# Gated linear attention and a bilinear feed-forward network on one core: blocks of 256 tokens by two rows, full-width loads, two states per block, gaps and two chunks' decay by matmuls, a reordered start

## The chip, the core and the metric

The kernel runs on one core of one Trainium2 chip. The metric is the device time of one execution in microseconds (us). A run is called fast if it lies within 1.5% of the fastest of its kernel, and only fast runs are compared. The profile is of one execution; its span is shorter than the time of the same execution, by 1.7 us for the kernel before (232.1 against 233.83).

TensorE does the matmuls, VectorE, ScalarE and GpSimd the elementwise work, SyncE and GpSimd issue the loads. Sixteen DMA engines carry the data. Each engine works through its instructions in order; that matters for everything below (in the changed kernel ScalarE stands 8.40 us for one late load, with ready work behind it).

## The reference

```python
for t in range(S):                                  # B=4, H=8, S=768, D=48
    state = alpha[:, :, t, :, None] * state + einsum('bhd,bhe->bhde', k[:, :, t], v[:, :, t])
    y[:, :, t] = einsum('bhd,bhde->bhe', q[:, :, t], state)
x = y.transpose(0, 2, 1, 3).reshape(3072, 384)
return (x @ w_a) * (x @ w_b) @ w_out                # 384 -> 1536 -> 384
```

The kernel computes the recurrence in blocks: the logarithm of alpha, a prefix sum of it by matmul, scaled keys and queries, masked scores inside a block, and a state carried from block to block. In the text a *chunk* is 512 tokens, of which there are six. Its feed-forward part is 24 groups of three 128x512 matmuls and an output product of 48 matmuls (`ff_a`, `ff_b`, `ff_o`). The schedule places the attention of chunk c+1 between the feed-forward groups of chunk c, by hand.

## The kernel before: what the change touches

The schedule is a list of stages for the start, and for each chunk a list of (step, chunk, stage): the stage is emitted behind that feed-forward group. `ld` loads, `L` is the logarithm, `A` the prefix sum and its exponentials, `dec` brings the decay at a block's end to the state's layout, `mk`/`mq` scale keys and queries, `C` transposes, `D` makes the masked scores, `Y` is the product with the values, `K` updates the state, `v` casts the values, `W`/`Wo` load weights. The letter at the end names the engine (V VectorE, P GpSimd, S ScalarE, Y SyncE).

```python
START = [ ...
    (0, "ld k 1 YP"), (0, "ld q 1 YP"), (0, "ld v * YP"), ...
    (0, "gate_w k"), (0, "W 0 256"), (0, "W 256 768"), (0, "W 768 1536"),    # weights wait for chunk 0's k
    (1, "gate_in a"), (1, "ld a * YP"), (1, "ld k 0 YP"), (0, "Wo 0 4"), ...   # then chunk 1
    (0, "ff 0 0"), (0, "ff 1 0"), (0, "Y 1 S dma"), (0, "ff 2 0"), ... ]
def _steady(c):
    n, m = c + 1, c + 2
    return _ld(0, m) + [(0, n, "C 0 0 V"), ... (18, n, "Y 1 S dma"), (18, n, "fill YY"), (20, n, "K 1"),
            (18, m, "L * P"), ... (25, m, "dec"), ...]
...
def load(ch, what, us, engs):                       # two DMAs, 64 partitions each
    for g in range(2):
        bs = slice(2 * g + us.start, 2 * g + us.stop)
        engs[g].dma_start(out=t[g * HC:(g + 1) * HC, us]..., in_=src[bs, :, ch.c * C:(ch.c + 1) * C, :]...)
...
def stY(ch, u, eng, how="dma"):
    if ch.c > 0:                                    # state product: full-array, block-diagonal state
        for p in range(P2):
            for g in range(2):
                nc.tensor.matmul(y[:, g, p, :], lhsT=Sb[:, 2 * g + u, p, :], rhs=..., ...)
    ...
    if ch.c > 0 and how == "pe":                    # gap rows by matmul (chunk 1 only)
        evac(KT, P2); ...; evac(0, KT)
def fill(ch, engs):                                 # gap rows by DMA (later chunks)
    for t in range(KT):
        for r in range(2):
            engs[r].dma_start(out=ch.xT[r * DP + D:(r + 1) * DP, t], in_=ch.xT[r * DP + t * G:..., KT])
```

(Cuts are marked by dots.) The heads are 48 wide and lie in tiles of 64 rows; the 16 "gap" rows are filled from the fourth pair of heads, so that three full 128-row tiles make the 384 columns of x.

## Time and profile before

| | kernel before |
|---|---|
| median of 4 runs | 233.28 us (231.94 to 233.68) |
| span of the profiled run | 232.1 us |
| TensorE busy | 205.6 us, 89% |
| first feed-forward group of chunk 0 | 23.54 us |
| first full-width group of chunk 1 | 70.69 us |
| steady period of a chunk | 31.95 us |

The two times in the middle: the first says when TensorE's main work begins, the second (I call it T1) when the start is over.

### The profile page before, as it was taken

What the parts mean: (1) busy time and instruction counts of PE and PEld (TensorE: products, weight loads), DVE (VectorE), ACT (ScalarE), POOL (GpSimd) and SP (SyncE); (2) the same over time, 40 slices, a digit from 0 to 9 for tenths busy, and PEclk for the clock granted to TensorE, in tenths of its full rate; (3) what the DMA queues carried; (4) which work ended last, traced back from release to release, by engine and by line L of the source; (5) the groups of instructions that cost most, each with busy time, mean ns of one, the idle gap of its engine ahead of it and who ended that gap; (6) DMA issues with size and microseconds to landing.
All of it is one profiled execution on the core that took longest, in us unless ns stands there. A gap on an engine that the chain in (4) does not pass through costs nothing.

```text
span 232.1 us, 5488 instructions
## 1 busy us (share of the span) xinstructions
PE 205.6 (89%) x2238; PEld 116.2 (50%) x2238; DVE 119.6 (52%) x174; ACT 120.1 (52%) x192; POOL 86.3 (37%) x96
## 2 busy tenths in 40 slices
PE   6488499497998879996999989999899999999992
PEld 6366364234664345562555555465455555644461
DVE  2676337335424758715588641977625875035500
ACT  3568334865537843838234777344793344234420
POOL 7558784157003890145901079202477000000000
PEclk9759979979999999999799999999999999999998
DMA  6999999995999319992399811699723000230023
GB/s 134 228 193 107 142 179 202 233 221 75 176 208 215 85 4 197 203 192 74 57 207 205 121 48 36 120 199 204 114 54 87 0 3 9 68 79 0 0 55 82
DMA packets 61584, 27.93 MB, mean 120 GB/s; under 512 B 53668, under 2 KB 60984, under 8 KB 61560
## 3 DMA queue, kind: packets, MB, share of 16 engines
q1 hardware_dynamic: 54440, 20.91, 54.5%
q0 software_dynamic: 5008, 5.90, 15.3%
q10 hardware_dynamic: 2112, 0.79, 1.9%
q8 instruction: 17, 0.28, 0.5%
q14 instruction: 7, 0.06, 0.1%
HBM read 25.98 MB, written 4.75 MB: 132 GB/s over the span
## 4 chain that ended last, share of the span: by engine, by line
PE 60%; DMA 16%; SPq 8%; ACT 5%; issue 4%; POOL 4%; DVE 1%; ACTq 0%; POOLq 0%; DVEq 0%
PE f L360 19%; PE f L351 15%; PE f L343 14%; SPq L164 6%; DMA v_t<-in_v_dram 5%; DMA k_t<-in_k_dram 4%; PE f L229 3%; PE s L247 3%; DMA wb_t<-in_moe_w_b_dram 2%; DMA wa_t<-in_moe_w_a_dram 2%; PE y L260 2%; PE y L266 2%; PE f L200 2%; DMA a_t<-in_alpha_dram 1%; ACT la L178 1%
## 5 line engine op out<-in xcount | busy, mean ns | idle before, releaser
L351 PE MATMUL f<-xT,wb_t 128*128 128x512 bf16 (+1 forms) x225 | 61.5, 384 | 2.8 <-DMA wb_t<-in_moe_w_b_dram 2.8
L343 PE MATMUL f<-xT,wa_t 128*128 128x512 bf16 (+1 forms) x225 | 60.6, 378 | 3.4 <-DMA xT<-xT 2.0
L360 PE MATMUL f<-wo_t,prod 128*128 128x384 bf16 x288 | 49.5, 326 | 1.4 <-ACT as__2133 L345 0.6
L360 PEld LDWEIGHTS <-prod 128*128 128x128 bf16 x288 | 27.8, 98 | 21.8 <-issue 2.9
L343 PEld LDWEIGHTS <-wa_t 128*128 128x128 bf16 x225 | 22.3, 100 | 29.3 <-DMA xT<-xT 3.2
L248 DVE TENSOR_TENSOR m<-s,mask 128x1024 bf16<-128x1024 f32 x22 | 26.9, 1223 | 15.7 <-PE s L247 15.7
L351 PEld LDWEIGHTS <-wb_t 128*128 128x128 bf16 x225 | 19.9, 101 | 21.5 <-issue 5.0
L326 POOL TENSOR_TENSOR Sb<-tmp,bl 48x384 bf16<-48x384 f32 x16 | 14.7, 918 | 37.6 <-DVE tmp L325 37.0
L362 ACT ACTIVATE ot<-f 128x384 f32<-128x384 f32 x24 | 11.8, 491 | 28.3 <-PE f L360 28.1
L208 POOL TENSOR_TENSOR Kp<-k_t,invb 128x768 bf16<-128x768 f32 x10 | 18.1, 1814 | 18.1 <-ACT invb L204 7.7
L200 PE MATMUL f<-l,ut_f 128*128 128x384 f32 x24 | 12.8, 619 | 7.5 <-DVE l L180 6.9
L208 POOL TENSOR_TENSOR Qp<-q_t,beta 128x768 bf16<-128x768 f32 x10 | 18.5, 1847 | 0.0
L235 DVE COPY qk<-f 128x1024 bf16<-128x1024 bf16 x16 | 11.1, 692 | 14.0 <-PE f L229 13.9
L180 POOL TENSOR_TENSOR l<-la 128x768 f32<-128x768 f32 x4 | 7.3, 1813 | 23.5 <-ACT la L178 23.5
L287 ACT ACTIVATE xT<-y 128x1024 bf16<-128x1024 f32 (+2 forms) x14 | 12.2, 872 | 6.0 <-PE y L260 4.8
L201 DVE TENSOR_TENSOR le<-f,la 128x384 f32<-128x384 f32 x12 | 6.7, 557 | 15.8 <-PE f L200 15.6
L325 DVE TENSOR_TENSOR tmp<-s,Sb 48x384 f32<-48x384 f32 x16 | 8.9, 555 | 7.0 <-PE s L315 6.4
L229 PE MATMUL f<-ident,Qp 128*128 128x128 bf16 x96 | 10.0, 230 | 2.4 <-POOL Qp L208 2.1
L178 ACT ACTIVATE la<-a_t 128x1536 f32<-128x1536 f32 (+1 forms) x7 | 9.1, 1302 | 4.4 <-DMA a_t<-in_alpha_dram 4.3
L247 PEld LDWEIGHTS <-qk 64*64 64x64 bf16 x384 | 6.6, 109 | 8.1 <-issue 3.1
L229 PE MATMUL f<-ident,Kp 128*128 128x128 bf16 x96 | 9.8, 227 | 0.7 <-DVE Kp L208 0.7
L247 PE MATMUL s<-qk 64*64 64x128 bf16 x352 | 9.3, 225 | 0.9 <-ACT qk L233 0.7
(219 smaller groups left out, 265.7 us busy)
## 6 DMA issues: line engine op xcount, KB each, us to landing
out_dram<-ot SPq DMA_DIRECT2D x48, 96.0 KB, 2.2
k_t<-in_k_dram SPq DMA_DIRECT2D x20, 192.0 KB, 6.4
q_t<-in_q_dram SPq DMA_DIRECT2D x20, 192.0 KB, 7.4
v_t<-in_v_dram SPq DMA_DIRECT2D x9, 384.0 KB, 8.3
a_t<-in_alpha_dram SPq DMA_DIRECT2D x9, 384.0 KB, 5.0
wo_t<-in_moe_w_out_dram POOLq DMA_DIRECT2D x3, 384.0 KB, 13.6
k_t<-in_k_dram POOLq DMA_DIRECT2D x3, 192.0 KB, 9.2
q_t<-in_q_dram POOLq DMA_DIRECT2D x3, 192.0 KB, 11.8
```

What stands on the lines that cost most here:

```text
L164: engs[g].dma_start(out=t[g * HC:(g + 1) * HC, us].rearrange("p b h r d -> p (b h) (r d)"), in_=src[bs, :, ch.c * C:(ch.c + 1) * C, :].rea ...
L200: nc.tensor.matmul(p, lhsT=ut_f32, rhs=ch.l2[:, u].rearrange("p h d -> p (h d)"), start=True, stop=True)
L208: eng.tensor_mul(dst[ch.c % 2][:, u, :, :, :D], src[:, u].rearrange("p h r d -> p r h d"), by[:, u])
L229: nc.tensor.transpose(t[:, j, p, :, r, :], src[:, u, r, hp:hp + 2, :].rearrange("s h d -> s (h d)"), ident)
L247: nc.tensor.matmul(s2[g * HC:(g + 1) * HC, r, p, rk, :], lhsT=qk[rs, 1, p, g, rk * HC:(rk + 1) * HC], rhs=qk[rs, 0, p, g, :], start=True, ...
L248: nc.vector.tensor_mul(m.rearrange("p r a k s -> p (r a) (k s)"), s2.rearrange("p r a k s -> p (r a) (k s)"), maskn(4))
L287: nc.scalar.activation(out=o_, in_=i_, func=AF.Copy)
L326: nc.gpsimd.tensor_mul(so, tmp[rs], bl)
L343: nc.tensor.matmul(ap, lhsT=wa_t[:, kk, f * 128:(f + 1) * 128], rhs=ff_x(ch, us)[:, kk], start=(kk == 0), stop=(kk == KT - 1))
L351: nc.tensor.matmul(bp, lhsT=wb_t[:, kk, f * 128:(f + 1) * 128], rhs=ff_x(ch, us)[:, kk], start=(kk == 0), stop=(kk == KT - 1))
L360: nc.tensor.matmul(op, lhsT=ch.prod[:, f, m * C:(m + 1) * C], rhs=wo_t[:, f, :], start=(f == 0), stop=(f == NFF - 1))
L362: nc.scalar.activation(out=ot, in_=op, func=AF.Copy)
```

## The change

Its intent: loads of the full 128 partitions, an earlier start of chunk 1, fewer zeros in the state products, no small DMAs on the path, and scalings on the faster engine. The core of the diff, with cuts:

```diff
 START = [
-    (0, "ld a 0 YS"), ... (0, "gate_w k"), (0, "W 0 256"), ..., (1, "gate_in a"), (1, "ld a * YP"), ...
+    (0, "new"), (0, "ld a 0 Y"), (0, "L 0 V"), (1, "new"), (0, "ld a 1 Y"), (0, "ld q 0 Y"), (1, "gate_in a 0"), (0, "ld k 0 Y"), ...
+    (0, "ld v 0 Y"), (0, "ld k 1 Y"), ... (0, "ld v 1 Y"), (0, "W 0 512"), ... (1, "gate_in k 1"),
+    (0, "W 512 1536"), (1, "ld a * Y"), (0, "Wo 8 12"), ... (1, "ld q * Y"), (0, "dec P"), (1, "ld k * Y"), ...
+    ... (0, "C 1 0 V"), (0, "D 1 0 s2"), (0, "K 1 P y2"), (0, "ff 0 0"), (0, "S 1"), ...
 PLAN:
+    0: [(0, 1, "L * V"), (6, 1, "A 0"), (8, 1, "A 1"), (8, 1, "mk 0 V"), ..., (11, 1, "dec P"), ...
+        (16, 1, "K * P"), (16, 2, "new"), (17, 2, "ld a * P"), ..., (22, 2, "ld k * P"), (26, 2, "ld v * P"), (26, 2, "A 1")],
+    1: [(1, 2, "mq 0 V"), ..., (5, 2, "dec D"), ..., (13, 2, "K * P"), ..., (15, 2, "S 0"), ...
 def load(...):
-    for g in range(2): engs[g].dma_start(out=t[g * HC:(g + 1) * HC, us]..., in_=src[bs, :, ch.c * C:..., :]...)
+    eng.dma_start(out=t[:, us]..., in_=src[ch.b0 + us.start:ch.b0 + us.stop, :, ch.s * 2 * C:(ch.s + 1) * 2 * C, :]...)
+def decay_pe(ch):            # decay of a block by one-column matmuls, for chunks 0 and 1
+    nc.tensor.matmul(s2[r * DP:r * DP + D, g, e:e + 1], lhsT=ch.l2[gs, u, hd, :], rhs=one[gs], ...)
+def stS(ch, u):              # state products, 64x64, first half from S0, second from Sm
+    nc.tensor.matmul(y[rs, g, p, :], lhsT=Sm[...] if g else S0[...], rhs=queriesT(ch, u, p, g, rs), ...)
+def stG(ch, u, eng):         # gap rows by matmul, for every chunk
-def fill(...)                # gone
```

Chunks 2 to 5 get their decay through DRAM (`dec D`): the row is written out, and read back in the state's layout.

## The prediction

> **What bounds the kernel now.** I read the page first: the busy shares, then its forty slices. The core's TensorE is busy 89% of the span, no other engine over 52%.
>
> ```profile
> PE 205.6 (89%) x2238; PEld 116.2 (50%) x2238; DVE 119.6 (52%) x174; ACT 120.1 (52%) x192; POOL 86.3 (37%) x96
> ...
> PE   6488499497998879996999989999899999999992
> ...
> DMA  6999999995999319992399811699723000230023
> GB/s 134 228 193 107 142 179 202 233 221 75 176 208 215 85 4 197 203 192 74 57 207 205 121 48 36 120 199 204 114 54 87 0 3 9 68 79 0 0 55 82
> ```
>
> The span has two parts. In the first ten slices (58 us) the DMA engines are full and TensorE has holes; later the DMA has holes and TensorE is full. The chain of work that ended last, in order of time, agrees: loads and their issues up to about 56 us, then almost only matmuls.
>
> ```profile
> 0.74 3.43 DMA a_t<-in_alpha_dram
> 4.19 9.77 DMA k_t<-in_k_dram
> ...
> 30.05 0.68 SPq L164
> 30.77 0.67 SPq L164
> 31.48 2.42 SPq L164
> 33.94 3.57 SPq L164
> 37.56 3.63 SPq L164
> 41.23 2.95 SPq L164
> 44.23 11.84 DMA v_t<-in_v_dram
> ...
> 70.69 0.82 PE f L343 x3
> ...
> 107.71 0.59 SPq L303
> 108.34 1.81 DMA xT<-xT
> ...
> 132.24 0.87 ACT la L178
> ...
> 164.19 0.87 ACT la L178
> ...
> 219.94 7.81 PE f L360 x48
> 227.78 0.49 ACT ot L362
> ```
>
> Here chunk 1's loads enter the queue only from 30 us on (they are held behind the weights' issue), each issue takes up to 3.6 us, and the last v lands at 56 us. Chunk 1's feed-forward part starts at 70.69. The third thing to see is the fill of the gap rows by DMA at 105 to 110 us, which sits behind output stores in the same queue. What TensorE waited for, summed:
>
> ```profile
> PE f L200 <- DVE l L180: 6.9, 2, 3.5
> PE f L351 <- DMA wb_t<-in_moe_w_b_dram: 2.8, 1, 2.8
> PE f L229 <- POOL Qp L208: 2.1, 2, 1.4
> PE f L343 <- DMA xT<-xT: 2.0, 3, 0.9
> ```
>
> Durations from the timeline, start to next start, at full clock: a feed-forward group of three 128x512 matmuls takes 0.65 us, 24 of them 15.5 us (204.40 to 219.94); the output product of a chunk, 48 matmuls, 7.8 us. So a chunk's feed-forward costs 23.35 us and six cost 140. One chunk's attention on TensorE: two prefix sums at 0.65, four transpose groups at 0.45, four score groups at 0.35, two state products at 0.54, two value products at 0.56, two state updates at 0.37: 7.45 us. A steady period is 164.19 - 132.24 = 31.95, so 31.95 - 23.35 - 7.45 = 1.15 us of it is stall. From 70.69 to 227.75 there are 157.1 us; five feed-forwards (116.75) and four attentions (29.8) make 146.55, so 10.5 us there are stalls, most of them before 113 us. From the first feed-forward group (23.54) to 70.69 there are 47 us for about 31 of work: 16 us lost. That is 26 us to be won, with no work removed.
>
> **What the Trainium skill says.** "TensorE: Matmul & The Clock Gate", section Back-to-back issue gap, gives N/2.4 + 2.5 ns: 216 ns for 512 columns. The trace agrees (0.65 us for three). "TensorEngine Tiling (Array Packing)", section Overview, says that a 64x64 split works as four independent tiles. The trace agrees: 16 score matmuls of 64x64 by 128 columns take 0.35 us, eight full-array ones of the same width 0.54 us. "GPSIMD Engine Reference", section 4.1, puts two-input elementwise work on GpSimd at about twice VectorE's time; here the same 128x768 multiply is 1815 ns on GpSimd and 950 ns on VectorE. "DMA: Bandwidth & Descriptors", section Rules for kernel authors, says that two transfers to disjoint partition halves share the same engines, and to use one 128-partition transfer. This kernel's halves don't test it; so I count no higher rate for the wider loads, only fewer issues.
>
> **The change part by part.** (1) A chunk becomes 256 tokens of two rows instead of 128 tokens of four. Bytes, run length (two tokens, 384 bytes) and matrix shapes stay. Each token load covers 128 partitions: half the issues. Before's SPq issues of up to 3.6 us were such halves.
>
> (2) The order of the start. Chunk 1's loads are no longer held until the weights are issued at 30 us; in the order listing they follow chunk 0's in the same queue, held only by short memsets that stand before and after the first weight pieces. I estimate 6 to 12 us instead of 30 to 44. Weights come earlier too (first columns before, not after, chunk 0's keys have landed). The sum of bytes for chunks 0 and 1 and all weights is the same.
>
> (3) Each chunk now has two sequential halves: the state ahead and the state within it. The update must come before the state product: a longer chain (update, two or three VectorE operations of about 0.55 us, state product). Chunk 0 has it in the open: about 2 us more, against one row's data being enough for its first half. I leave its first feed-forward group at 24 us (before: 23.5).
>
> (4) State products: 16 tiles of 64x64 replace eight full-array ones: 2 x (0.35 - 0.54) = -0.4 us a chunk. The block-diagonal zeros and chunk 0's special value matrix go.
>
> (5) Gaps by matmuls: 12 a chunk. Six took 0.43 us (62.05 to 62.48) in chunk 1 before, so +0.85 us a chunk. The 24 small fills by DMA go, with the stall at 105 to 113 us. Attention is then 7.45 - 0.4 + 0.85 = 7.9 us.
>
> (6) Chunks 0 and 1 get their decay from 32 one-column fp32 matmuls. fp32 prefix sums show two passes per instruction in the trace; 64 passes at some 40 ns, an estimate from the small tiles' 22 ns and the slower fp32 weight load (234 against 98 ns), are 2.5 us. Chunk 0's lies in a wait, chunk 1's on TensorE's path.
>
> (7) Key and query scalings go from GpSimd (20 x 1.82 us) to VectorE (0.95 us). VectorE's sum in a period: 12 x 0.69 products, 4 x 1.22 masks, 4 x 0.95 scalings, 2 x 0.56, transposes, states, one copy and one cast about 5: 23 us of 31. Not a bound. It takes away the 2.1 us wait for Qp. GpSimd issues the later loads instead.
>
> **The sum.** From 24 us, the eight narrow feed-forward halves (8 x 0.66) and the second row's attention (2.9) reach 32 us. Then 16 full groups (10.4), chunk 1's attention with its decay (7.9 + 2.5), chunk 2's prefix sums (1.3) and the output product (7.8): chunk 1's feed-forward starts at 62 instead of 70.7. After it: 5 x 23.35 = 116.75; attention 4 x 7.9 - 1.3 = 30.3; stalls at 1 us a period, 4 (before: 10.5); from the last matmul to the end 232.1 - 227.75 = 4.35. 155.4 in all. 62 + 155.4 = 217.4; I say 217 us. So about 8.7 us come from the start and 6 from the middle.
>
> **The rivals.** *The start stays bound by DMA.* The bytes are the same and the engines were full to 52 us. If chunk 1's values land at 50, then VectorE, ScalarE and TensorE, which work in order, wait for them: the cast of v stands after 14 of 24 groups. Behind it are 8 groups (5.2), most of the attention (6), prefix sums (1.3), output (7.8) and the cast (1.5): 22 us, so 72 + 155 = 227, hardly a win. For it: the DMA row. Against it: the rate was not at its best (107 and 142 GB/s in slices 4 and 5, 233 in slice 8); and the placement itself. In before's schedule the logarithm stood at group 16, when alpha landed at 42 us, and the casts at 20 and 22, when v landed at 53 and 56. Now they stand at 0 and 14, which in my walk is 32 and 41 us. A tuned schedule would not stand so early if the data came at 50. I give this 15%.
>
> *New stalls in the middle.* The longer state chain, one bank pair for scores and one for outputs, and VectorE at 74% in order could cost 2 to 3 us a period more: 225 to 229. For it: before's periods were tight. Against: the state update is placed several groups ahead of its use. 10 to 15%.
>
> *More is won.* With no stall at all the floor is 24 + 140.1 + about 41 of attention + 4.35 = 209.5.
>
> **Range and chances.** Floor and first rival give 209 to 227. Faster by over 2% means below 228.3: both rivals have to hold to miss it, or a fault that I don't see: 0.91. Within 2%: 0.07. Slower: 0.02.
>
> **What would show it.** Right: chunk 1's first full-width feed-forward group at 58 to 66 us; no xT fill and no wait on it; periods of 31 to 32.5 us; the last matmul some 4 us before the end; token loads of chunk 1 landing by 42 us. Wrong: a wait of TensorE or ScalarE for v or alpha over 4 us between 30 and 60 us (first rival); waits of the state products for VectorE or GpSimd in the periods (second); the one-column matmuls over 4 us; VectorE over 85% in a period.

## More of the kernel before

The prediction shows the main lines. Two more lines of the page belong beside the later ones: the clock granted to TensorE in tenths, by fortieths of the span, and the number of DMA packets.

```profile
PEclk9759979979999999999799999999999999999998
DMA packets 61584, 27.93 MB, mean 120 GB/s; under 512 B 53668, under 2 KB 60984, under 8 KB 61560
```

From the tenth slice on the clock is at nine tenths or more in all slices but two, and most packets (53668 of 61584) are short: a run of two tokens of a head is 384 bytes.

## The result and the profile after

The changed kernel is slower: 248.94 us (247.5 to 249.36, 4 runs) against 233.28. The ratio is 1.0684, with a 95% interval of 1.0621 to 1.0747. (A ratio here is the mean time of one kernel's fast runs over that of the other's in the same rounds, so not quite the ratio of the medians.) The prediction said 217, within 209 to 227.

First the page of the changed kernel, to be laid beside the prediction's first fence: TensorE's busy tenths, its clock, and what the DMA moved.

```profile
PE   7756087399999893499999999999999999999992
PEclk9965559889999999589999999999999999999999
GB/s 176 247 207 187 163 205 257 169 1 4 186 108 258 235 266 234 4 166 223 65 65 3 254 254 75 69 0 3 4 34 99 0 3 3 32 96 0 3 48 81
```

A slice is 6.14 us (the span of 245.7 us by 40). From the 18th slice on (104 us) TensorE is full to the end. Before that it has three holes: in the fifth slice (25 to 31 us), the eighth (43 to 49 us), and the 16th and 17th (92 to 104 us). The clock is at half from the fourth to the sixth slice, and again in the 17th. The DMA engines stand still in the ninth and tenth (49 to 61 us), and are crowded from 74 to 98. The waits of TensorE name the three holes (us in total, times, longest; L328 is the state update in front of the first feed-forward group, L291 the state product, L206 the prefix sum):

```profile
PE y L328 <- ACT xT L298: 7.5, 1, 7.5
PE y L291 <- POOL Sm L342: 7.2, 1, 7.2
PE f L206 <- DVE l L186: 3.9, 1, 3.9
```

No line has the fill of the gap rows any more, as intended. The chain of work that ended last says what is behind each wait; its columns are start, length, and what.

```profile
8.76 20.21 DMA v_t<-in_v_dram
28.99 0.84 ACT vx L191
32.13 0.76 PE f L359 x3
...
43.62 1.28 ACT L184
44.91 1.49 ACT la L184
46.42 0.97 DVE l L186
47.44 1.32 PE f L206 x2
...
89.82 10.68 DMA bl<-row
101.55 0.95 PE y L291 x13
102.50 1.40 PE f L359 x3
```

The first hole: a v of chunk 0 (384 KB) takes 20.21 us, ScalarE waits for it, and the copy of xT that the first feed-forward group reads stands behind ScalarE's cast of that v. The second: a table load, the logarithm of chunk 1's alpha and an addition run one after the other, and TensorE's prefix sum waits at the head of its queue. The third: chunk 2's decay goes out to DRAM and back, and 3 KB take 10.68 us to come back; then a feed-forward group takes 1.40 us in place of 0.65, since the clock has dropped. GpSimd's timeline shows where the standstill of the DMA comes from:

```profile
60.29 0.82 POOL L342 TENSOR_TENSOR S<-tmp,bl 128x384 bf16<-128x384 f32 x1 [26.66 <-DVE tmp L341]
61.06 1.22 POOL L170 DMA_DIRECT2D a_t<-in_alpha_dram  x1
```

The loads of chunk 2 are issued by GpSimd, behind a state multiply that waits for VectorE; the first of them goes out at 61.06. What comes later agrees with the prediction. The windows between first groups of chunks 1 to 4 (window, length, busy time of TensorE's matmuls, its weight loads, VectorE, ScalarE and GpSimd, then clock, DMA share and GB/s):

```profile
79.19:123.20 44.01, 35.35 (x411) 19.54 (x419) 24.65 (x33) 21.99 (x37) 12.86 (x11) 0.92 0.67 171
123.20:154.41 31.21, 30.69 (x377) 16.92 (x385) 21.42 (x29) 19.73 (x32) 7.83 (x6) 1.00 0.57 130
154.41:186.90 32.49, 31.86 (x388) 18.00 (x394) 20.57 (x28) 19.78 (x32) 0.00 (x0) 1.00 0.14 27
```

Two of the three periods are inside the predicted 31 to 32.5 us, with VectorE at 20 to 21 us. Only chunk 1's is 44. So the loss is in the first half, and it can be laid out along the prediction's own sum:

| piece (us of the span) | predicted | changed kernel | difference |
|---|---|---|---|
| to chunk 0's first feed-forward group | 24 | 32.07 | +8.1 |
| narrow halves and the second row, to 43.34 | 8 | 11.27 | +3.3 |
| wait for chunk 1's prefix sum | 0 | 4.10 | +4.1 |
| full groups and chunk 1's attention, to T1 | 30 | 31.75 | +1.75 |
| T1 | 62 | 79.19 | +17.2 |
| T1 to the last matmul (241.33) | 151.05 | 162.14 | +11.1 |
| last matmul to the end | 4.35 | 4.4 | 0 |

### The profile page after: what moved, and what is told of

Its sections match the earlier page's. It is cut to its first block, busy times and chain, and to the rows that moved or that the text cites. A ratio compares the mean times of both kernels' runs of the same rounds, so it can differ in the third digit from the quotient of the medians.

```text
span 245.7 us, 5987 instructions
## 1 busy us (share of the span) xinstructions
PE 209.7 (85%) x2552; PEld 124.2 (51%) x2582; DVE 131.0 (53%) x187; ACT 124.5 (51%) x207; POOL 47.0 (19%) x67
## 4 chain that ended last, share of the span: by engine, by line
PE 59%; DMA 17%; ACT 7%; issue 6%; SPq 4%; DVE 3%; POOL 1%; POOLq 0%; DVEq 0%; ACTq 0%
PE f L378 16%; PE f L359 15%; PE f L369 15%; DMA v_t<-in_v_dram 8%; DMA bl<-row 4%; SPq L170 3%; DMA k_t<-in_k_dram 3%; PE f L206 2%; DMA row<-beta 2%; PE s L280 2%; PE f L253 2%; PE y L291 2%; PE y L307 1%; ACT la L184 1%; PE s L328 1%
## 5 line engine op out<-in xcount | busy, mean ns | idle before, releaser
L253 PE MATMUL f<-ident,QKp 128*128 128x128 bf16 x192 | 15.2, 227 | 1.3 <-DVE QKp L214 1.2
L257 ACT ACTIVATE kqT<-f 128x1024 bf16<-128x1024 bf16 x13 | 13.2, 1020 | 5.2 <-PE f L253 5.1
L253 PEld LDWEIGHTS <-QKp 128*128 128x128 bf16 x192 | 12.7, 102 | 5.0 <-DVE QKp L214 1.4
L298 ACT ACTIVATE xT<-y 128x256 bf16<-128x256 f32 (+1 forms) x18 | 10.4, 575 | 9.6 <-PE y L307 7.8
L206 PE MATMUL f<-l,ut_f 128*128 128x384 f32 x24 | 11.4, 560 | 4.0 <-DVE l L186 3.9
L280 PE MATMUL s<-kqT 64*64 64x128 bf16 x384 | 12.8, 239 | 1.5 <-DVE kqT L259 1.4
L291 PE MATMUL y<-kqT,Sm 64*64 64x128 bf16 x96 | 7.9, 240 | 7.2 <-POOL Sm L342 7.2
L214 DVE TENSOR_TENSOR QKp<-k_t,invb 128x768 bf16<-128x768 f32 x12 | 11.3, 952 | 2.5 <-DMA k_t<-in_k_dram 2.5
L280 PEld LDWEIGHTS <-kqT 64*64 64x64 bf16 x384 | 8.7, 115 | 6.7 <-DVE kqT L259 3.3
L214 DVE TENSOR_TENSOR QKp<-q_t,beta 128x768 bf16<-128x768 f32 x12 | 11.4, 950 | 0.0
L259 DVE COPY kqT<-f 128x1024 bf16<-128x1024 bf16 x11 | 7.5, 686 | 5.2 <-PE f L253 5.2
```

The lines of the kernel that those rows point to most:

```text
L206: nc.tensor.matmul(p, lhsT=ut_f32, rhs=ch.l2[:, u].rearrange("p h d -> p (h d)"), start=True, stop=True)
L214: eng.tensor_mul(dst[ch.c % 2][:, u, :, :, :D], src[:, u].rearrange("p h r d -> p r h d"), by[:, u])
L253: nc.tensor.transpose(t[:, j, r, p], src[:, u, r, hp:hp + 2, :].rearrange("s h d -> s (h d)"), ident)
L257: nc.scalar.activation(out=o_, in_=i_, func=AF.Copy)
L280: nc.tensor.matmul(s2[g * HC:(g + 1) * HC, r, p, rk, :], lhsT=keysT(ch, u, 2 * h + p, g, r, rk), rhs=queriesT(ch, u, 2 * h + p, g, rs), st ...
L291: nc.tensor.matmul(y[rs, g, p, :], lhsT=lhsT, rhs=queriesT(ch, u, p, g, rs), start=(p == 0), stop=False, skip_group_check=True)
```

## The experiments

My theory (A) was that four placements in the schedule cause the loss: the weights that share the DMA with chunk 0's v, the early place of the prefix sum, chunk 2's loads behind GpSimd's work, and chunk 2's decay through DRAM. The rivals were that a hole is only a symptom, so that closing it moves the wait elsewhere, and that the new parts themselves (gaps by matmul, narrower or wider loads) cost or bring more than I counted. Every experiment starts from the changed kernel unless it says otherwise, all results were correct, and the ratio is to the kernel before in the same rounds. Differences in us are of medians, of rounds whose kernel before had medians of 233.0 to 234.6, so the ratios are the safer measure. (Two runs of the kernel before, 406.32 and 236.06 us, were slow and are left out of the ratios. The single mends ran in two rounds on two chips, so a difference of a microsecond between them means little.)

| run | time, us (range of 4 runs) | ratio (95%) | T1, us |
|---|---|---|---|
| changed kernel | 248.94 (247.5 to 249.36) | 1.0684 (1.0621 to 1.0747) | 79.19 |
| decay of chunk 2 by matmul | 239.94 (239.67 to 240.96) | 1.0256 (1.0182 to 1.0331) | 79.20 |
| chunk 2's loads early | 243.34 (240.86 to 243.85), 3 fast runs | 1.0365 (1.0254 to 1.0477) | 79.48 |
| v's cast late | 248.57 (247.73 to 249.41) | 1.0617 (1.0538 to 1.0695) | 79.73 |
| weights held for v | 241.1 (239.81 to 242.27) | 1.0279 (1.0184 to 1.0375) | 74.39 |
| prefix sums later | 244.64 (242.96 to 245.58) | 1.0471 (1.0397 to 1.0545) | 76.07 |
| before, gaps by matmul | 241.68 (241.09 to 241.95) | 1.0349 (1.0291 to 1.0407) | – |
| four mends | 231.76 (231.17 to 232.73) | 0.9931 (0.9869 to 0.9994) | 73.43 |
| loads ranked | 226.42 (225.36 to 226.79) | 0.9684 (0.9615 to 0.9753) | 68.13 |
| ranked, logarithm earlier | 227.57 (226.98 to 227.96) | none | 68.14 |
| ranked, decay through DRAM | 229.45 (228.18 to 229.97) | none | 67.33 |
| ranked, half-width loads | 231.4 (230.81 to 232.61), 3 fast runs | none | 73.99 |

The last three ran on one chip together; there three of the four runs of the kernel before were slow (235.53 to 235.63, one at 231.76), so no ratio is given and the three are compared with each other.

### Decay of chunk 2 by matmul

```diff
-    1: [..., (5, 2, "dec D"), ...
+    1: [..., (5, 2, "dec P"), ...
```

> Only chunk 2's decay is taken from matmuls instead of the round trip through DRAM. Theory A (the wait at 94.5 to 101.5 us is the decay transfer bl<-row, 10.9 us behind bulk loads; it also cost clock after the 7 us of idle TensorE): the state product no longer waits, chunk 1's period falls from 44 us to 34 to 36, the time from 248.9 to 238.5 to 241. Rival B (the keys and values of chunk 2 come too late anyway, so the wait only moves to them): gain under 4 us, time over 245.

Measured: 239.94 us, 9.0 less. The wait of the state product for Sm (7.2 us) is gone from the waits, chunk 1's period is 35.7 us (79.20 to 114.92), T1 is unchanged, and the other holes are as they were. The gain is larger than the wait, as the groups at a lowered clock behind it went too. So the round trip is a cause of its own, and it lies in the middle, not in the start.

### Chunk 2's loads early

```diff
     (0, "ff 0 1"), (0, "ff 1 0"),
+    (2, "new"), (2, "ld a * Y"), (2, "ld q * Y"), (2, "ld k * Y"), (2, "ld v * Y"),
 ]
-    0: [... (16, 2, "new"), (17, 2, "ld a * P"), (19, 2, "ld q * P"), (22, 2, "ld k * P"), (26, 2, "ld v * P"), ...
```

> Chunk 2's four loads go to the SyncE queue right behind chunk 1's instead of GpSimd's, where they stand behind a state multiply. Theory A (the DMA stood idle at 49 to 61 us because GpSimd, in order, waited 26.7 us for a VectorE result before it could issue them; the crowd of loads at 61 to 95 us follows from it, and with it the late keys, values and decay of chunk 2): the DMA hole closes, the waits for k, v and bl of chunk 2 shrink, the decay's transfer takes under 5 us, time 238 to 243. Rival B (chunk 3's loads simply take the freed place ahead of the decay's transfer): gain under 4 us, over 245.

Measured: 243.34 us in its fast runs, 5.6 less. The DMA moves 264 and 211 GB/s in the ninth and tenth slices, where it had moved 1 and 4, and stands still only afterwards, from 60 to 72 us. T1 did not move, but the wait for Sm shrank from 7.2 to 2.5 us, although the decay still went through DRAM: its read took 5.59 us, over the 5 expected. The two mends so far cure the same wait from two sides: the small read is slow where bulk loads stand before it.

### V's cast late

```diff
-    (0, "Y 0 S"), (0, "v 1 S"), (0, "C 1 1 S"), (0, "G 0 S"), (0, "C 1 0 V"), (0, "D 1 0 s2"), (0, "K 1 P y2"), (0, "ff 0 0"), ...
+    (0, "Y 0 S"), (0, "C 1 1 S"), (0, "G 0 S"), (0, "C 1 0 V"), (0, "D 1 0 s2"), (0, "ff 0 0"), (0, "ff 3 0"), (0, "ff 2 0"), (0, "ff 1 0"),
+    (0, "v 1 S"), (0, "K 1 P y2"), (0, "S 1"), ...
```

> ScalarE's cast of row 1's v, and row 1's state update, go behind the first row's gap and four narrow feed-forward halves. Theory A (ScalarE in order blocks the first row's ready work at 21.8 to 31.5 us while it waits for v): the first feed-forward matmul stands at 22 to 24 us instead of 32.1, four halves (2.6 us at full clock, more at a low clock) fill the hole, time 3 to 5 us less: 244 to 246. Rival B (the first columns of the weights land no earlier than 29 us, so the hole stays): first feed-forward after 29 us, time within 1.5 us of 248.9.

Measured: 248.57 us: nothing. This is a miss of my expectation. The four narrow groups did move ahead of the wait, but v landed as late as before, and the second row's chain behind it is as long:

```profile
23.88 0.82 PE L359 MATMUL f<-xT,wa_t 128*128 128x256 bf16 x3
...
30.74 0.84 ACT L191 ACTIVATE vx<-v_t 128x768 bf16<-128x768 f32 x1 [2.26 <-DMA v_t<-in_v_dram]
31.63 0.64 PE L328 MATMUL y<-vx,QKp 64*64 64x48 bf16 x32 [3.24 <-ACT vx L191]
```

The first group is at 23.88 and T1 at 79.73. To fill a hole with work that would otherwise stand behind it helps only if something else than the late datum ends that stretch. Here the datum ends it: the state update that reads v starts at 31.63, against 31.50 in the changed kernel. The first hole is a symptom; v's landing is the cause.

### Weights held for v

```diff
-    (0, "W 512 1536"), (1, "ld a * Y"), ...
+    (0, "gate_w v 1"), (0, "W 512 1536"), (1, "ld a * Y"), ...
```

`gate_w` is a one-element GpSimd copy of the named tile, which stands in front of the weights' issue until the tile has landed.

> The second part of the weights is issued only when row 1's v has landed. Theory A (that v took 20.2 us because the weights share the DMA engines with the token loads): v lands at 20 to 24 us instead of 29.0, the first feed-forward matmul comes at 24 to 27 instead of 32.1, time 243 to 247 unless the later weights become the next wait. Rival B (one queue with 128-partition loads is slow on its own): v lands within 2 us of 29.

Measured: 241.1 us, 7.8 less. V's cast starts at 20.56, and the first group at 23.45, where the prediction had put it (24):

```profile
20.56 0.84 ACT L191 ACTIVATE vx<-v_t 128x768 bf16<-128x768 f32 x1 [0.56 <-DMA v_t<-in_v_dram]
```

The wait of 7.5 us is gone. (The gate also holds the output weights, which GpSimd issues behind; the run doesn't tell the two apart.) But chunk 1's keys came later, VectorE waited 4.7 us for them and TensorE 3.1 for VectorE, and of the 8.6 us that the first group moved, T1 kept 4.8:

```profile
45.40 0.96 DVE L214 TENSOR_TENSOR QKp<-k_t,invb 128x768 bf16<-128x768 f32 x1 [4.72 <-DMA k_t<-in_k_dram]
```

The Trainium skill, "DMA: Bandwidth & Descriptors", section Issuing engines are not separate DMA queues, says that DMAs from any engine end on the same 16 DMA engines and interleave. This pair of runs agrees: v is loaded by SyncE and the weights by GpSimd, and v landed at 20.56 or 28.97 us according to whether those weights were out.

### Prefix sums later

```diff
-    0: [(0, 1, "L * V"), (6, 1, "A 0"), (8, 1, "A 1"), (8, 1, "mk 0 V"), (9, 1, "mq 0 V"), (10, 1, "mk 1 V"), (11, 1, "dec P"), ...
+    0: [(0, 1, "L * V"), (10, 1, "A 0"), (12, 1, "A 1"), (11, 1, "mk 0 V"), (12, 1, "mq 0 V"), (13, 1, "mk 1 V"), (13, 1, "dec P"), ...
```

> Only chunk 1's prefix sums (and what follows from them) move behind one more feed-forward group each. Theory A (the 3.9 us hole at 43.5 to 47.4 us is not a late load but ScalarE's table load and logarithm with the prefix sum right behind them in TensorE's order): the hole closes to under 1 us, time 244.5 to 246.5. Rival B (the weights or alpha are late there, so TensorE waits for them instead): hole stays in another name, time within 1.5 us of 248.9.

Measured: 244.64 us, 4.3 less, with T1 3.1 earlier; the wait for the addition shrank from 3.9 to 2.1 us at its longest. I had read step 6 as "behind six feed-forward instructions". The plan skips the groups that the start has done already; these are the two groups of each of the first four column blocks, so steps 0 to 7 are empty in chunk 0, and the prefix sum stood directly behind the start. For the same reason the edit moved the first prefix sum behind three full groups, not behind one more.

### The kernel before, with gaps by matmul

```diff
-  (10, n, "Y 0 S dma"), ... (18, n, "Y 1 S dma"), (18, n, "fill YY"), ...
+  (10, n, "Y 0 S pe"), ... (18, n, "Y 1 S pe"), ...
```

> The kernel before with one part of the change alone: gap rows by matmuls for all chunks, no fills by DMA. By the prediction's part 5: the stall at 105 to 113 us (4 to 5 us) goes, 10 more matmul groups of 0.43 us come (about 4 us over chunks 2 to 5): 231 to 234 against 233.3. Rival (the matmuls wait for ScalarE's copy of the gap rows each time, 1 us per half chunk, on TensorE's path): 237 to 242.

Measured: 241.68 us, 8.7 more than the kernel before beside it. The prediction had credited this part with a gain. TensorE's wait for the copy ahead of the gap matmuls, in the kernel before and in this one (us in total, times, longest):

```profile
PE y L293 <- ACT xT L287: 1.0, 2, 0.5
```

```profile
PE y L293 <- ACT xT L287: 4.9, 10, 0.5
```

That is 0.49 us each time, plus 0.43 us of matmuls: 8 more of them are 7.4 us, of the 8.7. The fill's own waits (2.0 us) went; behind T1, which hardly moved (70.86), the profiled run took 7.3 us longer, so some 2 us there are not accounted for. In the kernel before the gap matmul follows its value product at once and TensorE stands through ScalarE's copy. In the changed kernel a group lies between, and such waits remain only in the start. So this part is not good in itself; it needs the placing that came with it.

### The four mends together, then the loads ranked

The four mends are the edits above, without the late cast. The ranked kernel adds an order of the loads by who needs them first:

```diff
-    (0, "W 512 1536"), (1, "ld a * Y"), (0, "Wo 8 12"), ... (0, "gate_w q 0"), (0, "Wo 0 4"), ... (0, "Wo 4 8"), ... (1, "ld v * Y"), ...
+    (0, "gate_w v 1"), (0, "W 512 1536"), (1, "gate_in q 1"), (1, "ld a * Y"), ... (1, "ld v * Y"), (1, "gate_w k 1"), (0, "Wo 8 12"), (0, "Wo 0 4"), (0, "Wo 4 8"), ...
```

The output weights (1536 x 384 x 4 bytes, 2.36 MB) are not read before chunk 0's output product. In the changed kernel they were issued among and ahead of chunk 1's tokens.

> Together: chunk 2's decay by matmuls (alone -9.0), chunk 2's loads early (alone -5.3), second part of the weights held for v (alone -7.8), prefix sums later. If the three waits are one after another and independent, about 248.9 - 9 - 8 - 4, less an overlap of most of the 5.3: 226 to 230. If the DMA work of the start (about 13.4 MB to read until chunk 1's values are in) is the floor under all of them, they overlap: chunk 1's feed-forward part does not start before 70 us and the time is 231 to 236.

> As the one with four mends, and the loads are ranked by first use: chunk 0, second part of the weights, chunk 1's q, k, v, then the output weights. If ranking is what the start lacks: chunk 1's keys no longer late (45 us with the weights held alone), 3 to 5 us better than the four mends, 222 to 228. If the DMA floor decides: within 2 us of it.

Measured: the four mends give 231.76, level with the kernel before, with T1 at 73.43. That is what the expectation had for a floor by bytes. The ranked loads give 226.42, which beats both (0.9684 of the kernel before), with the same bytes and T1 at 68.13: so it was the order and not the floor. The gains of the single mends add up to 26.7 us and together give 17.2. In the profiled runs T1 moved by 5.8 us (4.8 and 3.1 alone: each moves the end of the start only as far as the next late datum), and the rest of the span shrank by 9.7 (8.7 and 6.9 alone: the round trip and the loads cure the same wait). In the ranked kernel no wait of TensorE is over 2.1 us, and from T1 to the last matmul (220.56) it takes 152.4 us.

```profile
PE f L207 <- DVE l L187: 3.8, 2, 2.1
```

### What is left of the start: the logarithm earlier

```diff
-    (0, "ff 2 1"), (0, "ff 0 1"), ...          0: [(0, 1, "L * V"), (10, 1, "A 0"), ...
+    (0, "ff 2 1"), (1, "L * V"), (0, "ff 0 1"), ...          0: [(10, 1, "A 0"), ...
```

> The ranked-loads kernel (226.42 us) with chunk 1's logarithm put into the start, two narrow groups earlier. In that kernel TensorE still stands 2.08 us before chunk 1's first prefix sum, for the addition behind the logarithm, and ScalarE waits up to 2.4 us for alpha. If the logarithm's place is what is left there: 224.3 to 225.5 us, wait for the addition under 1 us. If alpha's landing is the limit: 226 to 227, the same hole under another name.

Measured: 227.57 us, no gain: the span of the profiled run is 225.0 as in the ranked kernel, T1 68.14 against 68.13. (The ranked kernel was not run again beside it.) The wait for the addition is gone, and this has come in its place:

```profile
PE f L360 <- ACT as__707 L364: 1.9, 1, 1.9
```

ScalarE now does its table load and logarithm (2.8 us) ahead of the copies that free the accumulation banks, and a feed-forward group waits for those. The hole is the same under another name, though not for the cause that I had put down: alpha had landed; it is ScalarE's order. Together with the late cast this is the second run where a wait only moved.

### The decay through DRAM, without the crowd

```diff
-    1: [..., (5, 2, "dec P"), ...
+    1: [..., (5, 2, "dec D"), ...
```

> The ranked-loads kernel with chunk 2's decay through DRAM again, as in the changed kernel. Theory A (the round trip costs because its 3 KB transfers stand behind bulk loads; in the ranked kernel the loads of chunk 2 are over when the row is issued, at about 72 us, though chunk 3's begin): the row lands within 5 us, 226 to 229 us, wait of the state product under 2 us. Theory B (the round trip in itself is too long for its place, five groups ahead): wait of 5 us or more, 231 to 235 us.

Measured: 229.45 us, 1.9 above the run with the earlier logarithm beside it. That run differs in the logarithm too, but has the ranked kernel's span and T1; the profiled span is 2.2 above that of the ranked kernel. The state product waits 2.5 us, between the two expectations and nearer to A's. The two transfers in the chain:

```profile
71.28 4.94 DMA row<-beta
76.77 5.83 DMA bl<-row
```

The read takes 5.83 us where it took 10.68. In the changed kernel the median of all such reads is 2.3 us and the least 2.0. So the round trip is dear by what stands before it in the DMA, and even in this lighter traffic it is not free.

### The width of the loads by itself

```diff
-    eng.dma_start(out=t[:, us]..., in_=src[b0 + us.start:b0 + us.stop, :, ch.s * 2 * C:(ch.s + 1) * 2 * C, :]...)
+    for g in range(2):
+        lo = (2 * ch.s + g) * C
+        eng.dma_start(out=t[g * HC:(g + 1) * HC, us]..., in_=src[b0 + us.start:b0 + us.stop, :, lo:lo + C, :]...)
```

> The ranked-loads kernel with every token load cut into two of 64 partitions, one per row half: part 1 of the change undone alone, bytes and order kept. The prediction's view (width brings only fewer issues): 226 to 227.5 us. Rival (the wide load is a faster load: 253 GB/s were written in the changed kernel where the kernel before had 233 at best): chunk 1's v lands 3 to 5 us later than 45.6, and the time is 229 to 232 us.

Measured: 231.4 us in its fast runs, 3.8 above the run with the earlier logarithm beside it; the profiled span is 5.8 above that of the ranked kernel. T1 is 73.99, 5.9 later. The first group of chunk 0 starts at 27.84 instead of 24.64, behind a wait of VectorE for chunk 0's keys (2.27 us). The cast of chunk 1's v starts at 50.03 instead of 45.62, but waits for no load in either run, so it doesn't say when that v landed. The DMA rates of the first 50 us in slices of 1.25 us, first of the ranked kernel:

```profile
GB/s 0 63 285 281 261 262 260 262 240 209 236 194 189 177 263 261 270 119 167 193 174 154 185 149 185 152 156 244 261 262 261 261 261 268 268 239 210 204 204 204
```

and of the one with half-width loads:

```profile
GB/s 0 20 243 220 206 206 207 203 209 177 197 208 169 178 164 205 217 196 195 187 193 191 160 182 161 181 160 190 184 191 193 188 193 201 182 200 201 190 195 203
```

Where only token loads run (the sixth to eighth slices), the wide ones hold 260 to 262 GB/s and the halves 203 to 207. Over the 50 us that is 10.62 against 9.18 MB, with nine packets in ten under 512 bytes in both. The Trainium skill, "SBUF — State Buffer", section Door 1: The DMA port swizzle, says that bandwidth depends on how many of 16 ports the partitions reach, and that partitions 0 to 63 reach only eight. This run agrees in direction; the loss is a fifth, not a half. It doesn't tell the partitions from the size, since each half-load also has half the bytes.

## Why the prediction was wrong, and where it was right

**Two steps of the sum failed.** The first is the start: "I leave its first feed-forward group at 24 us", together with the sentence that defended it, "A tuned schedule would not stand so early if the data came at 50". I had named the right rival, that the start stays bound by DMA, had seen for it that the bytes are the same and the engines full, and gave it 15% on an inference from where stages stand in a list. The placement proved nothing: chunk 1's v landed at about 48 us (issued at 39.09, landed 9.3 us later), though the list had it cast at 41 in my walk. Nor did the rival go far enough: it let only chunk 1's values be late, with 227 us. No engine waited for those, because an earlier load was late already: ScalarE's cast of chunk 0's v waited until 28.97, and the first group came at 32.07. With the weights held it was at 23.45.

**The second is the middle**, "stalls at 1 us a period". From T1 on the changed kernel took 11.1 us more than the sum, and chunk 2's decay alone is 9.0 of the time (part 6 below).

**The signs.** I had asked for a wait of TensorE or ScalarE for v or alpha of over 4 us between 30 and 60 us. None came: ScalarE's 8.40 us for v ended at 28.99, and TensorE's 3.94 was for the addition behind the logarithm. The sign of the second rival did come, a state product that waited 7.2 us for GpSimd; but what GpSimd waited for was the decay's transfer, not the longer state chain.

**Chunk 1's loads entering at "6 to 12 us"** was wrong too, though I called it an estimate. SyncE's instruction for chunk 1's q starts at 13.18 and takes 18.09 us; those for k and v start at 31.37 and 39.09.

```profile
13.18 18.09 SPq L170 DMA_DIRECT2D q_t<-in_q_dram  x1
```

I had read the order in the queue and not asked how long the queue lets an issue stand. The order change did not bring these loads forward; it brought weights in front of them.

**The prefix sum in the open** (+4.1) was a misreading of the schedule: I counted "16 full groups" with the logarithm beside them, and did not see that no group lies between the start and the prefix sum.

**Part 6 of the sum left out a term.** I priced the one-column matmuls of chunks 0 and 1 at 2.5 us; the 64 passes took 0.83 to 0.90. What I did not price at all is that chunk 2 keeps the way through DRAM, and has less time for it: the row goes out at step 5 and the state update needs it at step 13, eight groups later (ten before the state product), where the kernel before had 15 (steps 8 to 23). Its read landed after 10.68 us, where such reads took at most 2.5 in the kernel before. Taking it away gave 9.0 us. With part 7 it is the same: "GpSimd issues the later loads instead" has no cost in my text, and that is why the loads were crowded when the row had to come back (5.6 us by moving them).

**Part 5** was credited with a gain for taking the small DMAs away. The stall at their wait did go, but the kernel before with this part alone is 8.7 us slower. That the changed kernel doesn't pay this is the work of its placing.

**Part 1** was sized too low: "I count no higher rate for the wider loads". They are faster by a quarter (261 against 206 GB/s), and undoing them in the ranked kernel cost 3.8 us against the run beside it. The page that I quoted advised just this, and I set it aside since the kernel before could not test it.

**What held.** Periods of 31.21 and 32.49 us were predicted at 31 to 32.5; VectorE is no bound (20 to 21 us of a period); apart from the decay, the longer state chain brought no wait over 1.5 us; the fill's wait is gone. The middle's sum of 151.05 us is 152.4 in the ranked kernel. That kernel's time, 226.42, is inside my range, though not by the start that I had forecast: T1 is 68.13 in place of 62. Its shortfall against 217.4 is 6.1 there, 1.35 in the middle, and 1.4 to 1.8 because my sum was one of the profiled span, which leaves out that much of the time. I predicted, in effect, a version of this change with its loads in a better order, and took for granted that it was the one in the diff.

**What stays open.** That the narrow halves and the second row took 3.3 us longer than counted can be added up but was not tested: six of the sixteen narrow groups followed each other at 0.61 to 0.66 us where the later ones take 0.33 (1.9 us, at the lowered clock), and two waits for ScalarE's copy at the gap matmuls are 0.49 and 0.90. How much of the ranked kernel's start could still be won was not tried further: its DMA engines are at work almost without a break up to about 50 us.

## What to carry to other kernels

When a start is bound by loads, write down the bytes and the order in which they are needed, and ask of every transfer which earlier one it delays; where a stage stands in a tuned list is no evidence of when its data come. Look for small dependent transfers and for loads issued by an engine that also computes: here they cost 9.0 and 5.6 us, and the first had caused no wait in the profile before. A hole that is filled with other work is closed only if the late datum does not also end that stretch.

## What the Trainium skill lacked or had wrong

- "SBUF — State Buffer", section Door 1: The DMA port swizzle, gives 196 GB/s for 64 partitions against 328 for 128, both at 1 MiB, a loss of 40%. For the token loads here, in runs of 384 bytes and one half behind the other, it was 206 against 261 GB/s, a fifth.
- "DMA: Bandwidth & Descriptors", section Issuing engines are not separate DMA queues, calls the sequencer's time to start a DMA usually small beside the DMA itself. In the changed kernel one issue instruction of SyncE took 18.09 us, with the DMA engines full, and held the loads behind it.
- No page that I used tells what a small dependent transfer costs behind bulk loads. Reads of 3 KB landed after 2.0 us at the least, 2.3 in the median and 10.9 at the most in one execution.
